# A hand-laid instruction order replaced by another, with eight transfers at most under way, and w_out loaded in four pieces

## The chip, the core and the metric

The kernel runs on one core of a Trainium2 chip. The metric is device time in microseconds (us). The engines are PE (TensorE, matmuls), DVE (VectorE), ACT (ScalarE), POOL (GpSimd) and SP (SyncE, which issues all transfers here). Each runs its own list of instructions strictly in order and waits on semaphores for the others.

## What is computed

Windowed attention over 8 batches, 8 heads, 576 positions, 64 channels a head, and a gated layer on its result:

```python
scores = scale * np.matmul(q, k.transpose(0, 1, 3, 2))
rel = pos[:, None] - pos[None, :]
mask = (rel >= 0) & (rel < 64)
attn = softmax(np.where(mask, scores, -1e9))
x = np.matmul(attn, v)                       # heads side by side: 8 x 576 x 512
for k in range(5):
    gate_pre += conv_w[k] * xp[:, k:k + S, :]
gate = 1.0 / (1.0 + np.exp(-gate_pre))
out = (gate * (x @ w_val)) @ w_out
```

q, k and v are float32; w_val, conv_w and w_out arrive as 64-bit floats, whose two 32-bit words the kernel takes apart itself.

## The kernel before, in words

**Stages.** The work is cut into some 1,500 named pieces. A *pair* is two heads of one batch; `w` numbers groups of two pairs (16 of them, two to a batch), `g` the two halves of a group's query blocks (5 and 4 blocks), `hh` the head of the pair.

- Loads, on SP: `LQi` (q and k of pair i), `LVw` (v of group w, eight transfers), `LW0_0`, `LW0_1`, `LW1_0`, `LW1_1` (quarters of w_val, 512 KB), `LW2`, `LW3` (halves of w_out, 1 MB), `LC` (conv_w), `DO` (stores).
- Attention: `S(w,g)` (scores, PE), `M((w,g),hh)` (add the mask, take the minimum of the negated row, DVE), `X` (exponent and row sum, ACT), `R` (reciprocals, DVE), `N` (normalise; DVE, ACT or POOL), `T` (transpose, DVE), `AVw_0` to `AVw_10` (product with v, PE).
- Splitting of weights into a high and a low part: `w0` to `w3` from w_val, `w4` to `w7` from w_out, `cw` from conv_w; steps `h k b c H p u l r s` on DVE, ACT and POOL (so `w2h` is the first step of w_val's third quarter).
- x: `EXi` copies pair i's result out of PSUM, `XH`, `XL` split it into high and low part.
- Gate: `Ki_y` is the convolution of pairs 0 and 1 of batch 0 on PE (with the diagonals that `DG` builds), copied by `CC`; for all other pairs `Ci_4` is its first tap on ACT, `Ci_3` to `Ci_0` the others on DVE. `SIGb` is batch b's sigmoid, with a change of ACT's function table before and after it.
- Last layer: `Vb_half_jb` (12 matmuls, x by w_val), `HF` (times the gate, DVE), `HH`, `HL` (high and low part of it, ACT and POOL), `Orow` (12 matmuls, output tile), `EO` (copy out of PSUM).

PSUM has two "s" buffers (one S takes both), two "av" buffers (one AV takes both; they come free with `EX` in pairs 0 and 1, with the last tap in the others) and two "f" buffers for `K`, `V` and `O`.

**Order.** A long string, `ORDER`, lists every piece by name in the order in which its instructions are written out. A suffix `/A`, `/V`, `/G` picks ACT, DVE or POOL where there is a choice. A word `*5+0` puts five *spare* matmuls of the first kind (128 x 512, written to a buffer that nobody reads; each is two passes on PE) in front of the next piece, `*0+3` three of the second kind. `placed()` reads the string, and the last loop of the kernel emits the pieces one by one; each engine's list is what falls to it.

**Transfers.** Each transfer that SP issues signals one of eight semaphores, in turn. Before a semaphore is taken again SP waits until the transfer that had it has landed, so at most eight are under way and a transfer waits for the one eight places ahead in SP's list.

Of the kernel before, what the change touches and what calls it, by code (L numbers as in the profile page):

```python
# [54 lines left out]
X((1,0),1) w4u w3l/V R(0,1) w4k/V *1+0 S(1,1) N((0,1),1)/G T((0,0),1) M((1,1),1) N((0,1),0)/G T((0,1),1) w4b
M((1,1),0) T((0,1),0) *0+1 AV0_0 AV0_1 AV0_2 w3r/G w4c w3s/V w4p LQ4_0 LW3 LQ5_0 LV1 LW0_1 LQ6_0 LQ7_0 AV0_3
AV0_4 AV0_5 AV0_6 AV0_7 AV0_8 AV0_9 AV0_10 *0+3 S(2,0) X((1,1),0) w4l/V X((1,1),1) R(1,0) R(1,1) EX0/V DG1/G
w5h/A w4H N((1,1),0)/A EX1/A XH0/A w5u XH1/A N((1,0),1)/V w4r/V N((1,0),0)/V w4s/V M((2,0),0) T((1,0),1)
T((1,0),0) M((2,0),1) N((1,1),1)/G XL1 DG0/G XL0 FR0 FR1 K1_0 AV1_0 S(2,1) T((1,1),1) T((1,1),0) M((2,1),0)
M((2,1),1) K1_1 AV1_1 AV1_2 AV1_3 AV1_4 X((2,0),0) X((2,0),1) w1h/A X((2,1),0) CC1_0 X((2,1),1) AV1_5 AV1_6  # L60
AV1_7 AV1_8 AV1_9 AV1_10 w1k/V R(2,0) w5k/V w1b w5b w1c N((2,0),0)/V w5c w1p w5p T((2,0),0) R(2,1) K0_1 S(3,0)
w1H CC1_1 EX2/A EX3/A C2_4 XH2/G C3_4 CC0_1 XH3/A N((2,0),1)/A w1l/V C2_3 M((3,0),0) C3_3 M((3,0),1) K0_0
T((2,0),1) C3_2 S(3,1) M((3,1),0) M((3,1),1) LV2 LQ8_0 LQ9_0 LV3 S(4,0) X((3,0),0) w5H w5l/G w1r/G XL3
N((2,1),1)/G XL2 w1s/G w5r/G w5s/G N((2,1),0)/G LQ10_0 LQ11_0 V0_1_1_0 X((3,0),1) X((3,1),0) CC0_0 X((3,1),1)
w6h/A w7h/A C2_2 C3_1 C2_1 R(3,0) C2_0 T((2,1),1) C3_0 N((3,0),1)/G N((3,0),0)/G M((4,0),0) T((2,1),0) R(3,1)
M((4,0),1) w6k/V w7k/V w6b w7b SIG0_0 w6c w7c HF0_1_1 w6p w7p FX1 FX0 AV2_0 AV2_1 AV2_2 AV2_3 AV2_4 AV2_5 AV2_6
AV2_7 AV2_8 AV2_9 AV2_10 V0_0_2_0 S(4,1) V0_0_3_0 T((3,0),1) HF0_0_2 M((4,1),1) HF0_0_3 T((3,0),0) EX4/A w6u
EX5/A C5_4 w7u C4_4 LV4 LQ12_0 LQ13_0 N((3,1),0)/G HH0_1_1_0/G HL0_1_1_0 w6l/G HH0_0_2_0/A HH0_0_3_0/A HL0_0_3_0
HL0_0_2_0 w7l/G V0_0_0_0 C4_3 M((4,1),0) HF0_0_0 C5_3 C4_2 X((4,0),0) w6H w7H V0_1_0_0 V0_0_1_0 S(5,0) HF0_1_0
# [1014 lines left out]
```

## Time and profile before

| | us |
|---|---|
| median of 3 runs (lowest, highest) | 329.29 (329.21, 330.62) |
| the profiled execution, as timed | 331.42 |
| its span, first to last instruction | 329.6 |
| PE busy | 313.0 |
| DVE busy | 260.3 |
| ACT busy | 246.0 |
| POOL busy | 174.0 |

The rows of the trace are from the profiled execution; its own time is 2.13 us above the median and 1.8 above its span. "Busy" adds up instructions; matmuls overlap and their ends are modelled, so a busy PE is not PE at its peak.

### The profile page before, as it was taken

Reading aid. Unit: us, or ns where it says so; the run is one execution under the profiler, and the core shown is the slowest. Engines: PE = TensorE matmul, PEld = TensorE weight load, DVE = VectorE, ACT = ScalarE, POOL = GpSimd, SP = SyncE. Lnnn points to the kernel's source line nnn. Section 1 sums busy time; section 2 is a strip of 40 time slices with the busy share of each in tenths; the row PEclk is TensorE's granted clock in tenths of the full one; section 3 lists DMA queues with packets and bytes.
Section 4 is the critical chain, followed back from the end, with each engine's and each line's share of the span. In section 5 each row is a group of like instructions: output and inputs, shape, how many; then the busy total and the mean of one; then the engine's idle time right before and its main releaser. Section 6 shows DMA issues by size and latency. Waiting matters only on the chain.

```text
span 329.6 us, 14996 instructions
## 1 busy us (share of the span) xinstructions
PE 313.0 (95%) x6142; PEld 264.2 (80%) x6142; DVE 260.3 (79%) x992; ACT 246.0 (75%) x844; POOL 174.0 (53%) x227
## 2 busy tenths in 40 slices
PE   8966978899999999999999999999999999999996
...
PEclk9976879999999999999999999999999999999999
...
GB/s 229 384 131 291 254 234 136 96 196 33 37 177 196 193 169 122 184 183 152 148 126 191 110 105 189 183 157 2 140 114 116 30 69 64 34 66 32 2 96 95
DMA packets 28228, 45.03 MB, mean 137 GB/s; under 512 B 3968, under 2 KB 15488, under 8 KB 28160
## 3 DMA queue, kind: packets, MB, share of 16 engines
q1 hardware_dynamic: 28160, 44.08, 43.3%
...
HBM read 34.62 MB, written 9.44 MB: 134 GB/s over the span
## 4 chain that ended last, share of the span: by engine, by line
PE 80%; DVE 13%; ACT 5%; issue 2%; POOL 0%; ACTq 0%; POOLq 0%
PE o L918 29%; PE v L852 27%; PE av L610 10%; PE s L521 8%; DVE p L542 4%; DVE gp L808 3%; PE g L777 3%; PE spare L1032 2%; ACT p L552 2%; DVE pts L579 2%; ACT p L571 1%; ACT h_hi L241 1%; PE spare L1034 0%; DVE w4a L424 0%; ACT L552 0%
## 5 line engine op out<-in xcount | busy, mean ns | idle before, releaser
L552 ACT ACTIVATE p<-p,nm 128x96 f32<-128x96 f32 x288 | 103.9, 363 | 7.7 <-DVE nm L542 7.5
L808 DVE SCALAR_TENSOR_TENSOR gp<-av,cw,gp 128x575 f32<-128x575 f32 (+3 forms) x120 | 93.4, 802 | 7.5 <-ACT gp L811 6.7
L852 PE MATMUL v<-xl,wv_hi 128*128 128x288 f32 x256 | 77.6, 303 | 0.7 <-ACT ot L241 0.7
L852 PE MATMUL v<-xh,wv_lo 128*128 128x288 f32 x256 | 75.4, 294 | 0.0
L852 PE MATMUL v<-xh,wv_hi 128*128 128x288 f32 x256 | 75.0, 293 | 0.0
L881 POOL TENSOR_TENSOR h_lo<-hf,h_hi 128x288 fp32r<-128x288 f32 (+2 forms) x80 | 53.9, 690 | 23.5 <-ACT h_hi L241 22.0
L542 DVE CUSTOM_DVE_ANT_0 p<-s,mask 128x96 f32<-128x96 f32 x288 | 54.8, 250 | 7.3 <-PE s L521 7.1
L918 PE MATMUL o<-wo_hi,h_lo 128*128 128x512 f32 (+1 forms) x148 | 59.6, 403 | 0.2 <-DVE hf L863 0.2
L918 PE MATMUL o<-wo_lo,h_hi 128*128 128x512 f32 (+1 forms) x148 | 57.7, 390 | 0.0
L918 PE MATMUL o<-wo_hi,h_hi 128*128 128x512 f32 (+1 forms) x148 | 57.6, 389 | 0.0
L552 ACT ACTIVATION_READ_ACCUMULATOR p<-p,nm 128x1 f32 x288 | 54.2, 188 | 0.0
L852 PEld LDWEIGHTS v<-xl,wv_hi 128*128 128x128 f32 x256 | 48.1, 188 | 4.0 <-ACT ot L241 1.1
L760 POOL TENSOR_TENSOR xl<-x,xh 128x576 fp32r<-128x576 f32 x32 | 46.0, 1445 | 9.9 <-ACT xh L241 9.6
L246 POOL CAST h_hi<-hf 128x288 fp32r<-128x288 f32 (+2 forms) x37 | 14.2, 392 | 66.1 <-DVE hf L863 57.6
L852 PEld LDWEIGHTS v<-xh,wv_hi 128*128 128x128 f32 x256 | 48.2, 188 | 0.6
L852 PEld LDWEIGHTS v<-xh,wv_lo 128*128 128x128 f32 x256 | 48.1, 188 | 0.0
L610 PEld LDWEIGHTS av<-pts,v 32*64 32x64 f32 x2560 | 36.5, 135 | 11.3 <-issue 5.3
L610 PE MATMUL av<-pts,v 32*64 32x96 f32 (+2 forms) x2560 | 39.6, 251 | 6.1 <-DVE pts L579 2.7
L521 PEld LDWEIGHTS s<-ktb,qtb 64*32 64x32 f32 x2304 | 30.7, 108 | 17.4 <-issue 14.5
L521 PE MATMUL s<-ktb,qtb 64*32 64x96 f32 x2304 | 38.9, 255 | 5.2 <-issue 2.7
L863 DVE TENSOR_TENSOR hf<-v,gp 128x288 f32<-128x288 f32 x64 | 28.2, 447 | 18.0 <-PE v L852 13.9
L573 POOL TENSOR_TENSOR p<-p,rc 128x384 f32<-128x384 f32 (+1 forms) x30 | 28.5, 955 | 20.9 <-DVE rc L561 17.6
...
## 6 DMA issues: line engine op xcount, KB each, us to landing
...
st<-in_w_val_dram SPq DMA_DIRECT2D x4, 512.0 KB, 4.1
st<-in_w_out_dram SPq DMA_DIRECT2D x2, 1024.0 KB, 10.2
...
```

What stands on the lines that cost most here:

```text
L246: COPY = {"A": scopy, "V": vcopy, "G": lambda out, in_: nc.gpsimd.tensor_copy(out=out, in_=in_)}
L521: nc.tensor.matmul(sp_t[m, hh][z * Q:z * Q + Q, t, :], lhsT=held("qt", i)[r, c:c + Q], rhs=held("kt", i)[r, c:c + KW], start=True, stop=True)
L542: nc.vector.tensor_tensor_reduce(out=pe[:, t, :], in0=sp_t[u][:, t, :], in1=mask_of(w, n0 + t), scale=-SCALE, scalar=3.0e38, op0=ALU.add, ...
L552: nc.scalar.activation(out=pe[:, t, :], in_=pe[:, t, :], func=AF.Exp, scale=-1.0, bias=nm[:, t:t + 1], accum_out=su[:, t:t + 1])
L573: MUL[e](out=pe, in0=pe, in1=rc.unsqueeze(2).broadcast_to([P, ng, KW]))
L610: nc.tensor.matmul(av_t[w, z // 2][hh * D:(hh + 1) * D, c + lo * Q:c + hi * Q], lhsT=v_t[w][z * Q:z * Q + Q, hh, m % 2, m // 2 - KEYS[th][ ...
L760: SUB[e](out=batch_tile(xl_t, "xl", b, F32R)[:, hp, :], in0=x_t[i // 2][:, i % 2, :], in1=xh_t[b][:, hp, :].bitcast(F32))
L808: nc.vector.scalar_tensor_tensor(out=acc, in0=av(i, 0, S - back), scalar=col, in1=acc, op0=ALU.mult, op1=ALU.add)
L852: nc.tensor.matmul(vp_t[u][:, 0:NH], lhsT=w[:, c, js], rhs=x[:, c, hs], start=(a + z == 0), stop=(a + z == NM - 1))
L863: nc.vector.tensor_mul(out=hf, in0=vp_t.pop(u)[:, 0:NH], in1=gp_t[b][:, jb, hs])
L881: SUB[e](out=h_lo[:, jb, dst:dst + hi - lo], in0=hf_t[u][:, lo:hi], in1=h_hi[:, jb, dst:dst + hi - lo].bitcast(F32))
L918: nc.tensor.matmul(op_t[key][:, 0:cs.stop - cs.start], lhsT=h[:, jb, col:col + P], rhs=w[:, jb, cs], start=(a + z == 0), stop=(a + z == NM ...
```

## The change

The string `ORDER` is another one throughout: the same pieces, in another order, some on other engines, and with other spares. Each 1 MB load of w_out goes out as two transfers of 512 KB. A tuple `lane` is added to the settings; nothing in the kernel reads it. All arithmetic stays.

```diff
     low='NNNNNAAAA',
+    lane=(2200.0, 900.0, 700, 3350, 1.15),
 )
...
-LW1_0 LC LQ0_0 LQ1_0 *5+0 S(0,0) w2h/A w2k/V cwh/A cwk/V w2b cwb w2c cwc w2p cwp w2l/V cwl/V M((0,0),0)
...
+LW1_0 LC LQ0_0 LQ1_0 LW0_0 LW1_1 w2h/V LQ0_1 LQ1_1 w2k/V cwh/A cwk/V w2b cwb w2c cwc cwH w2H w2p cwp w2l/V LQ2_0
+*4+0 S(0,0) cwl/G M((0,0),0) X((0,0),0) w2r/G LQ3_0 M((0,0),1) w0h/V w0k/V w2s/V w0b X((0,0),1) *2+0 S(0,1) w0c
...
             else:
-                nc.sync.dma_start(out=sv[0], in_=src[:, 2 * (n % 2):2 * (n % 2) + 2, :])
+                for y in range(2):
+                    nc.sync.dma_start(out=sv[0][:, y, :], in_=src[:, 2 * (n % 2) + y, :])
```

On PE, the pieces from the first AV on stand like this, word by word from the two strings with everything of other engines left out. Before: `*0+1 AV0 *0+3 S(2,0) K1_0 AV1_0 S(2,1) K1_1 AV1_1..10 K0_1 S(3,0) K0_0 S(3,1) S(4,0) V0_1_1 AV2 V0_0_2 S(4,1) V0_0_3 V0_0_0`. After: `*3+0 AV0 *1+0 S(2,0) *2+0 S(2,1) AV1_0..1 K1_0 AV1_2..10 K0_1 S(3,0) K0_0 S(3,1) K1_1 S(4,0) V0_1_1 AV2_0..4 V0_0_2 AV2_5 S(4,1) AV2_6..10 V0_0_0 V0_0_3`. From there on V, O, S and AV alternate in much the same way in both.

Three places in the engines' lists follow. `DMAHW0` to `DMAHW7` are the eight semaphores.

SP's list around the loads of w_out (`st`), before: LW2, then `v` of LV0, `qtb`/`ktb` of LQ4, LW3, LQ5, and the first of LV1.

```order
L387 DMA st_131<-in_w_out_dram 128x2x1024 [waits DMAHW0_49]
L356 DMA v_276<-in_vw_dram 32x2x320 [waits DMAHW1_49]
...
L356 DMA v_276<-in_vw_dram 32x2x384 [waits DMAHW0_49]
L335 DMA qtb_77<-in_qT_dram 128x576 [waits DMAHW1_49,PE_49]
L336 DMA ktb_81<-in_kT_dram 128x576 [waits DMAHW2_49]
L387 DMA st_517<-in_w_out_dram 128x2x1024 [waits DMAHW3_49]
L335 DMA qtb_78<-in_qT_dram 128x576 [waits DMAHW4_49,PE_49]
L336 DMA ktb_82<-in_kT_dram 128x576 [waits DMAHW5_49]
L356 DMA v_521<-in_vw_dram 32x2x320 [waits DMAHW6_49]
```

And now, from LW2 to the two halves of LW3, which stand behind LV1:

```order
L389 DMA st_131<-in_w_out_dram 128x1024 [waits DMAHW0_49]
L389 DMA st_131<-in_w_out_dram 128x1024 [waits DMAHW1_49]
L357 DMA v_302<-in_vw_dram 32x2x320 [waits DMAHW2_49]
...
L357 DMA v_302<-in_vw_dram 32x2x384 [waits DMAHW1_49]
L336 DMA qtb_77<-in_qT_dram 128x576 [waits DMAHW2_49,PE_49]
L337 DMA ktb_81<-in_kT_dram 128x576 [waits DMAHW3_49]
L336 DMA qtb_78<-in_qT_dram 128x576 [waits DMAHW4_49,PE_49]
L337 DMA ktb_82<-in_kT_dram 128x576 [waits DMAHW5_49]
L385 DMA st_146<-in_w_val_dram 128x4x256 [waits DMAHW6_49]
...
L389 DMA st_879<-in_w_out_dram 128x1024 [waits DMAHW7_49]
L389 DMA st_879<-in_w_out_dram 128x1024 [waits DMAHW0_49]
```

LV0's last transfer waited for the one transfer of LW2 and now waits for LW2's second half; LW3 has moved from ahead of LQ5 to behind LV1.

DVE's list from the last step of w1 that it does (`w1l`) on, before: the first taps of pairs 2 and 3 (`gp`, from `av_0` and `av_1`), and the two mask groups of S(3,0), each of five instructions and their minima, of which the first is shown.

```order
L439 SCALAR_TENSOR_TENSOR w1l<-st_225,w1m 128x512
L808 SCALAR_TENSOR_TENSOR gp_815<-av_0_701,cw,gp_815 128x575
L542 ISA p_0_0_944,nm_0_0_943<-s_0_0_884,mask_89 128x96
...
L808 SCALAR_TENSOR_TENSOR gp_815<-av_1_702,cw,gp_815 128x575
L542 ISA p_0_1_952,nm_0_1_951<-s_0_1_885,mask_89 128x96
```

And now:

```order
L441 SCALAR_TENSOR_TENSOR w1l<-st_146,w1m 128x512
L810 SCALAR_TENSOR_TENSOR gp_902<-av_0_743,cw,gp_902 128x575
L581 STREAM_TRANSPOSE pts_1_915<-p_0_1_685 128x480
L810 SCALAR_TENSOR_TENSOR gp_902<-av_0_743,cw,gp_902 128x574
L544 ISA p_0_0_976,nm_0_0_975<-s_0_0_918,mask_89 128x96
...
L544 ISA p_0_1_983,nm_0_1_982<-s_0_1_919,mask_89 128x96
L581 STREAM_TRANSPOSE pts_0_996<-p_0_0_665 128x480
L810 SCALAR_TENSOR_TENSOR gp_902<-av_1_744,cw,gp_902 128x575
```

Between the first tap and the first mask group of S(3,0) now stand a transpose and pair 2's second tap, and pair 3's first tap has moved behind both mask groups.

ACT's list around the copies of AV1's result (`x<-av`, EX2 and EX3), before; `gp<-g` are the copies `CC`, `gp<-x,cw` the first taps.

```order
L552 ACTIVATE p_1_1_754,sums_65<-p_1_1_754,nm_1_1_753 128x96 x4
L448 CAST wv_hi<-w1a 128x4x128
L241 COPY gp_815<-g_1_759 128x288
L241 COPY x_928<-av_0_701 128x576
L241 COPY x_928<-av_1_702 128x576
L811 ACTIVATE gp_815<-x_928,cw 128x576 x2
L241 COPY gp_815<-g_1_878 128x288
L241 CAST xh_664<-x_928 128x576
L571 ACTIVATE p_0_1_684<-p_0_1_684,rc_0_862 128x96 x5
```

And now:

```order
L573 ACTIVATE p_0_1_685<-p_0_1_685,rc_0_784 128x96 x5
L554 ACTIVATE p_1_1_788,sums_65<-p_1_1_788,nm_1_1_787 128x96 x4
L242 COPY x_899<-av_0_743 128x576
L450 CAST wv_hi<-w1a 128x4x128
L813 ACTIVATE gp_902<-x_899,cw 128x576
L450 CAST wo_hi<-w5a 128x512
L242 COPY gp_902<-g_0_761 128x288
L242 COPY gp_902<-g_1_873 128x288
L242 COPY x_899<-av_1_744 128x576
L573 ACTIVATE p_0_0_665<-p_0_0_665,rc_0_784 128x96 x5
L813 ACTIVATE gp_902<-x_899,cw 128x576
L242 CAST xh_648<-x_899 128x576
```

Pair 2's copy and first tap now go ahead of the copies of the convolution on PE, and pair 3's come five pieces later than pair 2's.

## Rows read from the trace of the kernel before

**Rows 1.** The page: busy time of PE with its share of the span and its instructions; PE's busy tenths and its granted clock, in tenths of full speed, in 40 equal slices of the span (8.24 us each); the chain that ended last, by engine.

```profile
PE 313.0 (95%) x6142; PEld 264.2 (80%) x6142; DVE 260.3 (79%) x992; ACT 246.0 (75%) x844; POOL 174.0 (53%) x227
...
PE   8966978899999999999999999999999999999996
...
PEclk9976879999999999999999999999999999999999
...
PE 80%; DVE 13%; ACT 5%; issue 2%; POOL 0%; ACTq 0%; POOLq 0%
```

**Rows 2.** Busy time by stretches: from and to in us, the stretch's length, then busy us (and instructions) of PE, PE's weight loads, DVE, ACT and POOL, the granted clock of PE as a share of full speed, the share of the DMA engines and GB/s.

```profile
5.00:66.70 61.70, 50.76 (x1288) 35.15 (x1286) 53.89 (x253) 49.82 (x192) 30.06 (x28) 0.89 0.74 222
46.20:51.30 5.10, 5.10 (x101) 3.77 (x96) 0.84 (x3) 3.67 (x8) 3.22 (x4) 0.78 0.76 241
66.70:110.00 43.30, 43.22 (x893) 38.44 (x892) 40.28 (x160) 42.46 (x154) 34.69 (x44) 1.00 0.44 139
70.00:110.00 40.00, 39.92 (x868) 35.14 (x867) 36.98 (x146) 39.83 (x149) 31.59 (x41) 1.00 0.45 142
110.00:200.00 90.00, 89.74 (x2104) 77.80 (x2104) 82.65 (x331) 78.03 (x282) 51.36 (x65) 1.00 0.50 151
200.00:320.00 120.00, 119.09 (x1823) 105.63 (x1822) 80.44 (x235) 73.01 (x215) 55.10 (x77) 1.00 0.26 83
```

**Rows 3.** DVE in order of time: start, duration, instruction; in brackets the idle time before it and what ended that.

```profile
5.48 0.43 DVE L424 TENSOR_SCALAR w2a<-w2m 128x512 int32<-128x512 int32 x1
...
10.12 0.26 DVE L542 CUSTOM_DVE_ANT_0 p<-s,mask 128x96 f32<-128x96 f32 x1 [2.21 <-PE s L521]
...
15.77 1.17 DVE L424 TENSOR_SCALAR w3a<-w3m 128x512 int32<-128x512 int32 x1
...
37.96 1.03 DVE L579 STREAM_TRANSPOSE pts<-p 128x384 f32<-128x384 f32 x2
...
45.57 0.64 DVE L439 SCALAR_TENSOR_TENSOR w1l<-st,w1m 128x512 f32<-128x512 uint32 x1
48.34 0.82 DVE L808 SCALAR_TENSOR_TENSOR gp<-av,cw,gp 128x575 f32<-128x575 f32 x1 [2.12 <-ACT gp L811]
51.30 0.26 DVE L542 CUSTOM_DVE_ANT_0 p<-s,mask 128x96 f32<-128x96 f32 x1 [2.14 <-PE s L521]
...
65.99 0.45 DVE L863 TENSOR_TENSOR hf<-v,gp 128x288 f32<-128x288 f32 x1
```

**Rows 4.** The chain that ended last, in order of time, merged: start, duration, what. "issue" is time in which the engine waited for nothing that the profile shows.

```profile
1.44 7.54 PE spare L1032 x10
8.97 1.17 PE s L521 x67
...
41.78 1.14 PE av L610 x56
42.92 1.86 issue
44.78 1.76 PE av L610 x46
46.54 3.57 PE g L777 x10
```

**Rows 5.** ACT in order of time, as in rows 3.

```profile
46.45 1.18 ACT L241 COPY x<-av 128x576 f32<-128x576 f32 x2 [2.56 <-PE av L610]
...
59.61 0.67 ACT L413 ACTIVATE w6m<-st 128x512 f32<-128x512 f32 x1
...
61.02 1.28 ACT L995 ACT_TABLE_LOAD   x1 [0.18 <-DVE gp L808]
62.31 2.13 ACT L995 ACTIVATE gp<-gp 128x2304 f32<-128x2304 f32 x1
```

**Rows 6.** SP's issues in order of time (start, how long the issue took, which transfer); the time from issue to landing of the ktb loads issued before 6 us; and from the first 25 us the median time to landing of the loads of w_out and w_val.

```profile
3.18 0.43 SPq L336 DMA_DIRECT2D ktb<-in_kT_dram  x1
...
14.66 1.44 SPq L356 DMA_DIRECT2D v<-in_vw_dram  x2
...
20.84 0.56 SPq L356 DMA_DIRECT2D v<-in_vw_dram  x1
...
DMA to landing us min/median/max: 5.4/5.4/5.4
...
st<-in_w_val_dram SPq DMA_DIRECT2D x4, 512.0 KB, 4.1
st<-in_w_out_dram SPq DMA_DIRECT2D x2, 1024.0 KB, 10.2
```

**Rows 7.** PE: the first matmul of the third V product of batch 0 in order of time; then, from the chain, an AV alone, seven V products in a row and five output tiles (72 matmuls: 48 of 512 columns, and 24 of 256, since one tile is computed in two halves).

```profile
66.65 0.40 PE L852 MATMUL v<-xl,wv_hi 128*128 128x288 f32 x1
...
284.76 2.19 PE av L610 x113
...
301.54 11.04 PE v L852 x84
312.58 14.06 PE o L918 x72
```

**Rows 8.** The last `hf` multiplication on DVE and a subtraction `h_lo` on POOL, as in rows 3.

```profile
312.69 0.46 DVE L863 TENSOR_TENSOR hf<-v,gp 128x288 f32<-128x288 f32 x1 [1.11 <-PE v L852]
...
312.44 0.81 POOL L881 TENSOR_TENSOR h_lo<-hf,h_hi 128x288 fp32r<-128x288 f32 x1
```

More of the change, by code (lines that the diff above doesn't have):

```diff
@@ L55 @@
[L55 to L69, printed above, removed]
@@ new lines @@
+*1+0 S(1,0) M((1,0),0) M((1,0),1) X((0,1),1) cws/G w0r/G w0s/G X((1,0),0) *1+0 S(1,1) R(0,1) T((0,0),0) w3c CF
+M((1,1),0) T((0,0),1) N((0,1),0)/G N((0,1),1)/G T((0,1),0) LQ4_0 X((1,0),1) w3p T((0,1),1) M((1,1),1) R(1,0)
+DG1/G LQ5_0 *3+0 AV0_0 AV0_1 w3H w4h/A w3l/V w4k/V AV0_2 AV0_3 X((1,1),0) w3r/V AV0_4 AV0_5 AV0_6 w4b AV0_7
+AV0_8 w4c w3s/V AV0_9 AV0_10 DG0/V w4p w4u N((1,0),0)/A N((1,0),1)/A EX0/A *1+0 S(2,0) X((1,1),1) T((1,0),1)
+T((1,0),0) XH0/G w4l/G R(1,1) LW0_1 LV1 M((2,0),0) w4H w5h/A N((1,1),1)/G X((2,0),0) w5k/V w4r/V M((2,0),1)
@@ new lines @@
+N((1,1),0)/G XL0 w5u X((2,0),1) EX1/V *2+0 S(2,1) FR0 FR1 M((2,1),0) AV1_0 AV1_1 K1_0 AV1_2 w4s/V X((2,1),0)
+XH1/G XL1 T((1,1),1) T((1,1),0) R(2,0) M((2,1),1) w1h/A N((2,0),1)/A X((2,1),1) AV1_3 AV1_4 AV1_5 AV1_6 w1k/V
+w5b w1b w5c AV1_7 AV1_8 AV1_9 AV1_10 w1c w5p w1p R(2,1) w1l/V K0_1 LW3 LQ6_0 LQ7_0 LV2 LQ8_0 LQ9_0 EX2/A w1H
+C2_4 w5H LV3 C2_3 T((2,0),1) XH2/G S(3,0) CC1_0 CC0_1 EX3/A N((2,0),0)/A K0_0 C2_2 M((3,0),0) M((3,0),1) C3_4
+XH3/A X((3,0),0) T((2,0),0) C3_3 XL2 w1r/G N((2,1),1)/G T((2,1),1) w1s/G w5l/G XL3 w5r/G w5s/G N((2,1),0)/G
@@ new lines @@
+S(3,1) K1_1 CC0_0 X((3,0),1) M((3,1),0) X((3,1),0) M((3,1),1) C2_1 C3_2 w6h/A CC1_1 FX1 FX0 S(4,0) C2_0 C3_1
+R(3,0) LQ10_0 LQ11_0 V0_1_1_0 C3_0 N((3,0),0)/G X((3,1),1) w7h/A AV2_0 AV2_1 M((4,0),0) T((2,1),0) AV2_2 SIG0_0
+R(3,1) w6k/V w7k/V w6b M((4,0),1) N((3,0),1)/G AV2_3 AV2_4 V0_0_2_0 AV2_5 S(4,1) AV2_6 AV2_7 AV2_8 AV2_9 w7b
+AV2_10 LQ12_0 w6c w7c w6p w6u N((3,1),0)/G HF0_1_1 V0_0_0_0 w6l/G EX4/A w6H HH0_1_1_0/A T((3,0),0) HF0_0_2
+M((4,1),0) T((3,0),1) HL0_1_1_0 V0_0_3_0 EX5/A HH0_0_2_0/A C5_4 HF0_0_0 w7p M((4,1),1) w7H C4_4 V0_1_0_0 C5_3
@@ new lines @@
+w7u w6r/G HL0_0_2_0 HF0_0_3 C4_3 LV4 LQ13_0 HH0_0_3_0/A w7l/G V0_0_1_0 C5_2 C4_2 HL0_0_3_0 N((3,1),1)/G S(5,0)
+HF0_1_0 C4_1 X((4,0),0) X((4,1),0) HH0_0_0_0/A w7r/G HF0_0_1 C5_1 HH0_0_1_0/A C4_0 X((4,0),1) V0_1_3_0 V0_1_2_0
+C5_0 T((3,1),1) T((3,1),0) X((4,1),1) AV3_0 HL0_0_1_0 HL0_0_0_0 w7s/G AV3_1 R(4,0) HF0_1_2 AV3_2 AV3_3 AV3_4
+w6s/V AV3_5 AV3_6 AV3_7 AV3_8 AV3_9 AV3_10 N((4,0),0)/A HF0_1_3 HH0_1_3_0/A EX6/A HH0_1_2_0/A O128_0_0 R(4,1)
+M((5,0),1) N((4,0),1)/G HH0_1_0_0/G T((4,0),1) M((5,0),0) T((4,0),0) C6_4 EX7/A HL0_1_3_0 HL0_1_0_0 C6_3
@@ new lines @@
+HL1_0_0_0 HH1_0_3_0/G S(6,1) EO0_0/V C9_1 X((6,0),0) X((5,1),1) R(5,1) XH9/G C9_0 HF1_0_1 HH1_0_3_1/G XL9
+HH1_0_0_1/A HL1_0_3_0 N((5,1),0)/G HH1_0_1_0/A N((5,1),1)/A HH1_0_1_1/G HL1_0_3_1 HL1_0_0_1 V1_0_2_0 DO0_0
+LQ16_0 LQ17_0 LV6 X((6,0),1) T((5,0),0) M((6,1),1) M((6,1),0) V1_1_0_0 HF1_0_2 X((6,1),0) V1_1_2_0 HF1_1_0
+T((5,1),0) R(6,0) C8_2 HH1_1_0_0/A N((6,0),1)/A HL1_0_1_0 HH1_0_2_0/G HL1_0_2_0 HL1_0_1_1 HL1_1_0_0 HH1_0_2_1/G
+V1_1_1_0 S(7,0) HF1_1_2 C8_1 HH1_1_2_0/A V1_1_3_0 T((6,0),1) HF1_1_1 HL1_0_2_1 HL1_1_2_0 HH1_1_1_0/G HL1_1_1_0
@@ new lines @@
+AV7_9 AV7_10 S(9,1) V2_1_0_0 HH2_0_0_0/G HH2_0_1_0/G N((8,0),1)/G N((8,0),0)/G N((8,1),0)/A HH2_0_3_0/G
+HL2_0_0_0 X((9,0),0) HL2_0_3_0 HL2_0_1_0 EX14/V EX15/V T((8,0),0) T((8,0),1) M((9,1),0) HF2_1_0 T((8,1),1)
+V2_0_2_0 V2_1_2_0 X((9,0),1) X((9,1),0) C15_4 C14_4 HF2_0_2 M((9,1),1) R(9,0) HF2_1_2 N((9,0),0)/A HH2_1_2_0/A
+X((9,1),1) HH2_1_0_0/G HL2_1_0_0 HH2_0_2_0/G HL2_0_2_0 T((8,1),0) C14_3 V2_1_3_0 N((9,0),1)/G XH14/G XH15/A
+DO640_0 LQ20_0 LQ21_0 LV8 LQ22_0 LQ23_0 DO512_0 LV9 HF2_1_3 S(10,0) M((10,0),1) M((10,0),0) X((10,0),0) V2_1_1_0
@@ new lines @@
+HL3_0_1_0 HL3_0_2_0 HL3_0_2_1 HL3_1_0_0 AV9_5 AV9_6 AV9_7 AV9_8 AV9_9 AV9_10 T((10,1),1) EX18/V V3_1_2_0
+M((12,0),1) HF3_1_2 HH3_1_2_0/G HL3_0_1_1 HL3_1_2_0 V3_1_3_0 V3_1_1_0 C18_4 R(11,1) C18_3 C18_2 HF3_1_3
+HH3_1_3_0/G EX19/A X((12,0),0) C19_4 X((12,0),1) O1792_0_0 N((11,0),0)/A HL3_1_3_0 HF3_1_1 HH3_1_1_0/G HL3_1_1_0
+O2048_0_0 C19_3 C19_2 XH18/G XH19/A C18_1 C19_1 T((11,0),0) C18_0 C19_0 XL19 N((11,0),1)/A EO1792_0/A S(12,1)
+SIG4_0 AV10_0 AV10_1 AV10_2 EO2048_0/V R(12,0) LQ28_0 DO1792_0 DO2048_0 LV11 AV10_3 XL18 N((12,0),0)/G XL16
@@ new lines @@
+X((14,1),0) HF4_1_1 T((13,0),1) X((13,1),1) C22_1 C23_2 M((14,1),1) O2432_0_0 EO2432_0/A HH4_1_1_0/A CB4 FX11
+FX10 S(15,0) O2304_0_0 C23_1 C22_0 R(14,0) R(13,1) N((13,1),0)/V C23_0 HH4_1_3_0/A HH4_1_2_0/A HL4_1_2_0
+N((14,0),0)/A HL4_1_3_0 SIG5_0 HL4_1_1_0 AV12_0 AV12_1 AV12_2 T((13,1),0) AV12_3 EO2304_0/V AV12_4 DO2432_0
+DO2304_0 LV13 AV12_5 AV12_6 AV12_7 AV12_8 AV12_9 AV12_10 O2560_0_0 M((15,0),1) T((14,0),0) N((13,1),1)/G
+T((13,1),1) HF5_0_0 M((15,0),0) EX24/A N((14,0),1)/V C24_4 HH5_0_0_0/A C24_3 EX25/A C25_4 EO2560_0/A C24_2
@@ new lines @@
+HL5_0_2_1 V5_1_1_0 HF5_1_1 T((14,0),1) EX27/A V5_1_2_0 HL5_1_3_0 O2944_0_0 C27_4 C26_4 C26_3 C27_3 C26_2 XH26/A
+HF5_1_2 T((14,1),1) C26_1 M((15,1),0) C26_0 T((14,1),0) XL24 XH27/G C27_2 C27_1 C27_0 T((15,0),1) XL27
+HH5_1_1_0/A HH5_1_0_0/A EO2944_0/A HH5_1_2_0/A XL26 HL5_1_2_0 CB5 FX12 FX13 HL5_1_1_0 HL5_1_0_0 O2816_0_0
+EO2816_0/A DO2816_0 DO2944_0 V6_0_0_0 SIG6_0 O3328_0_0 AV14_0 AV14_1 AV14_2 EO3328_0/V AV14_3 AV14_4 AV14_5
+AV14_6 AV14_7 AV14_8 AV14_9 AV14_10 EX28/A HF6_0_0 V6_0_2_0 HF6_0_2 EX29/V O3200_0_0 V6_0_3_0 XH28/A X((15,1),0)
```

139 lines of the change are left out of this document (54 added, 85 removed).

## The prediction

> **What bounds the kernel now.** The page of the profile came first. TensorE (PE) is busy for 95% of the span and the chain that ended last runs on PE for 80% of it, but the 40 slices split the program in two [rows 1]: from slice 9 on PE reads 9 almost throughout, before that 6 to 9, with its granted clock down to 6 tenths. The table by stretches [rows 2] puts numbers on it. From 66.7 to 320 us PE lacks 0.08 + 0.26 + 0.91 = 1.25 us of 253.3: there nothing but fewer or shorter matmuls would help. In the first 66.7 us the reader should look at the DVE column instead: between 5 and 66.7 us it is busy 53.89 of 61.7 us, and 4.26 of the 7.8 us that it lacks lie in one stretch, 46.2 to 51.3. PE is no limit there, since it has time for filler matmuls (the "spares"). So the kernel is a start-up paced by DVE, then a long dense stretch paced by PE. The end moves with the moment at which the dense stretch starts.
>
> That moment can be named. The first two V products of batch 0 fill both "f" buffers of PSUM, so the third needs the first `hf` multiplication (HF0_1_1 in the order), which DVE starts at 65.99 [rows 3]; the third V product follows on PE at 66.65 [rows 7]. Ahead of it V0_1_1, V0_0_2, all of AV2 and S(4,1) are done. In the new order the third is V0_0_0, and ahead of it stands exactly the same set. So the difference of the two times for the third V product is the difference of the kernels, up to what changes inside the dense stretch.
>
> **The big gap.** After `w1l` (45.57) DVE waits 2.12 us for ScalarE (ACT) before C2_3 at 48.34, then 2.14 more for scores [rows 3]. The chain tells why [rows 4]: PE is in AV1 at 41.78, loses 1.86 us as "issue" in the middle of it, and ends it at 46.54; so ACT copies AV1 only at 46.45, after 2.56 us of waiting [rows 5]. AV1 began its second piece so late because K1_1 stood ahead of it. Then K0_1 takes 3.57 us [rows 4], at a granted clock of 0.78 in that stretch [rows 2], and S(3,0) sits behind it.
>
> **The change, part by part.**
>
> *Front.* The first spares are eight passes instead of ten; ten took 7.54 us, so PE would reach S(0,0) 1.5 us earlier. S(0,0) also needs the fourth q/k load, issued at 3.18, and a ktb load of these takes 5.4 us to land [rows 6]: 8.6, against 8.97 in the chain [rows 4]. A landing faster by 0.7 is possible, one that is no cover at all too. Gain 0 to 1.1, I take 0.7; DVE waits 2.21 us for just this [rows 3]. Its extra `w2h` (0.4 us) falls into that wait.
>
> *DVE's load up to HF0_1_1.* I compared the two lists of DVE instructions. Masked scores, reciprocals, transposes and convolution steps are the same 18, 8, 12 and 8 groups. Only before: two small pieces of conv_w, `w4l`, the copy EX0 and three normalisations; only after: `w2h`, `w2s`, `w3r`, DG0, EX1 and `w6p`. With 0.4 us for a one-input pass, 0.6 to 0.7 for a two-input one and 0.8 for DG0, which has no row (nearest: the tap of 575 elements) [rows 3], about 3.7 stand against 3.8: nothing, within 1 us either way.
>
> *The gap itself.* At C2_3 the new order has about 1.0 us less DVE work behind it (a transpose of 0.6 and some of the above come later). So DVE arrives at 46.2 - 0.7 - 1.0 = 44.5. Is C2_3 ready? The last transpose for AV1, T((1,1),0), ends at 39.0 now [rows 3]; it moves to 39.0 - 0.7 + 1.3 = 39.6, since 1.3 us more DVE work lies ahead of it. AV1's remaining nine steps now follow K1_0 directly and take at most the 2.2 us of a whole AV [rows 7], so they end at 41.8, not 46.5. ACT then has a half softmax piece to finish (to 42.0), EX2, `w1H` and the first tap: 42.0 + 0.6 + 0.6 + 0.8 = 44.0. So C2_3 starts at 44.5 without a wait. K0_1 still stands ahead of S(3,0): 41.8 + 2.6 (3.6 at half clock) + 1.2 = 45.6 to 46.6. That costs nothing only because C2_3, a transpose and C2_2 now cover it until 44.5 + 2.2 = 46.7; without that cover it would be the old 2.1 us. I keep 0.56 for handovers: the gap gives back 3.7 of its 4.26. Bounds: all 4.26; or 1.9, if the 1.86 of "issue" comes back inside AV1 and K0_0, whose cover is 1.8, runs at half clock.
>
> *From there to the third V.* HF0_1_1 would come at 65.99 - 4.4 = 61.6. It also needs the sigmoid, 1.28 of table and 2.13 [rows 5], after C3_0; that ended 0.18 before 61.02 [rows 5], so at 56.5 now, and the sigmoid at 59.9: covered by 1.7 us. On PE, AV2 is cut into pieces around V0_0_2 and S(4,1), and the last ends near 62.4. So the third V starts at 62.5, 4.1 us earlier than 66.65: 0.3 less than the 4.4.
>
> *SP's queue.* A transfer waits for the one eight places ahead. LV0's last piece was issued at 20.84, 4.7 us after the one before it, since it waited until the 1 MB w_out load had landed [rows 6]. The same bytes stand ahead of it now, so I give the two halves no gain: AV0 near 25 in both. The second w_out load moves from ahead of LQ5 and LV1 to behind them; `w6h`, the first to read it, ran only at 59.61 [rows 5]. Cost nothing; its cover is over 10 us.
> The Trainium skill, "DMA: Bandwidth & Descriptors", Rules for kernel authors, speaks against the split: for bandwidth it asks for 1 MiB or more per DMA. By its fit of 2.0 us plus bytes over 436 GB/s (Anatomy of one DMA; made on another issue path) two halves are an estimated 6.4 us against 4.4, and the sum would lose at most 2.0 if LV0's last piece held the path. The trace bears out neither figure: 512 KB landed in 4.1 us and 1 MB in 10.2.
>
> *Dense stretch.* The same products: V 11.04/7 = 1.58 us, output tiles 14.06/5 = 2.81, AV 2.19 [rows 7]. At the end, the second output tile after the last V now needs that V's `h`, while before the third did. The multiplication starts at 312.69 and takes 0.46; with a copy and a subtraction on POOL, at most 0.81 each [rows 8], that is 314.8, and the first tile (from 312.58) lasts to 315.4 [rows 7]. Hidden by 0.6. For new waits in 250 us I add 0.4 (bounds 0 to 3; now 1.25).
>
> **Sum.** The profiled execution took 331.42 us for a span of 329.6: 331.42 - 0.7 - 3.7 + 0.3 + 0.4 = 327.7. The median of the runs shown lies 2.13 below the profiled execution, which gives **325.6**. With every bound good (1.1, 4.26, 1.0 of DVE load) the gain is 6.4: 322.9. With every bound bad (0, 1.9, 1.0 lost, 0.3, 3) 2.4 are lost: 331.7.
>
> **Rivals.**
> *ACT sets the start, or new waits eat the gain (no change).* ACT is full from 70 to 110 us, 39.83 of 40 [rows 2]. Up to the sigmoid it gets 1.25 us more work: three normalisations and a copy come, a normalisation, a copy, two casts and `w2h` leave. With the idle time of now the sigmoid would end at 64.44 + 1.25 = 65.7 [rows 5] and the third V start at 66.2: 0.4 gained, 328.9. For it: that row. Against: before 61 us ACT's idle time is waiting for AV1 and masked scores, which come earlier. Chance 0.18.
> *More than the sum.* If "issue" and half clock vanish, and DVE also loses nothing more to its neighbours (a pass of 0.43 took 1.17 us at 15.77 [rows 3]), the upper bounds hold with that 0.7 on top: 322.2. Chance 0.08.
> *The dense stretch is not dense (slower).* Between HF0_0_0 and HF0_0_3 DVE now has `w7p`, a mask group and a tap, so 0.4 + 0.7 + 0.7 + 0.4 = 2.2 us from one `hf` to the next where V's pace is 1.58. If such an order goes on, PE waits 0.6 per V: after the seventh V the gain of 4.1 is gone, from the tenth on the kernel is over 0.5% slower, at the twelfth it is at 325.6 + 7.2 - 0.4 = 332.4. For it: DVE busy 40.28 of 43.3 us [rows 2]. Against: after batch 0 no weights are left to split. Chance 0.12.
> That the order moves nothing is excluded by the lists.
>
> **Chances.** What a measurement of this kernel can tell from no change is about 0.5%, 1.6 us. Forecast 0.62, more than the sum 0.08: faster 0.70. Same 0.18, slower 0.12. Range 322.3 to 329.8: it leaves out the farthest gain and most of the slower case.
>
> **What would show it.** Right: DVE idle between C2_3 and M((3,0),0) below 0.6; AV1 ending near 41.8; the third V of batch 0 at 62.5; PE idle below 2 us from there to 310. Wrong: AV1 ending after 44, a sigmoid that ends after 62, or PE waits for `hf` between 62 and 110 us.

## The result, and the profile after

The changed kernel is slower: 332.11 us against 330.18 (medians of 8 runs each), ratio 1.0063, interval 1.0034 to 1.0092. The ratio leaves out one run of the kernel before, 334.22 us, which ran in the chip's slower state. Forecast were 325.6 and "faster"; the range ended at 329.8. Yet the two profiled executions, 331.24 us (span 329.4) and 331.42 (span 329.6), show no loss at all. That contradiction is the first thing to explain.

The page of the changed kernel, with the lines that answer to [rows 1]:

```profile
PE 314.3 (95%) x6144; PEld 263.4 (80%) x6144; DVE 258.8 (79%) x985; ACT 245.4 (75%) x845; POOL 180.3 (55%) x241
...
PE   8695999899999999999999999999999999999996
...
PEclk9979699999999999999999999999999999999999
...
PE 77%; DVE 14%; ACT 3%; issue 3%; DMA 2%; SPq 0%; POOL 0%; ACTq 0%; POOLq 0%
```

The table by stretches of the changed kernel, columns as in [rows 2]; the last row runs from the third V product of batch 0 to the last output tiles:

```profile
5.00:66.70 61.70, 53.25 (x1307) 35.82 (x1306) 56.64 (x263) 52.23 (x203) 33.40 (x33) 0.92 0.74 229
46.20:51.30 5.10, 4.90 (x134) 3.46 (x136) 5.10 (x26) 5.10 (x15) 5.02 (x5) 1.00 0.71 201
66.70:110.00 43.30, 42.41 (x885) 37.47 (x885) 40.48 (x144) 40.90 (x151) 34.02 (x45) 1.00 0.49 144
110.00:200.00 90.00, 89.08 (x2095) 76.98 (x2095) 82.42 (x335) 76.67 (x277) 50.92 (x67) 1.00 0.48 144
64.30:311.93 247.63, 245.61 (x4781) 216.66 (x4782) 201.06 (x717) 191.95 (x642) 144.21 (x193) 1.00 0.39 118
```

DVE has no idle time left from 46.2 to 51.3 (5.10 of 5.10, before 0.84). But the dense stretch is less dense: PE lacks 0.89 us from 66.7 to 110 (before 0.08) and 0.92 from 110 to 200 (before 0.26), and from third V to last tiles 247.63 us pass. The same stretch of the kernel before is its row below:

```profile
66.65:312.40 245.75, 244.50 (x4785) 215.78 (x4781) 202.97 (x723) 192.04 (x646) 139.57 (x183) 1.00 0.38 118
```

In this pair the third V comes 2.35 us earlier (64.30 for 66.65, [rows 7]) and the rest takes 1.9 longer. DVE of the changed kernel in order of time, columns as in [rows 3]:

```profile
9.29 0.26 DVE L544 CUSTOM_DVE_ANT_0 p<-s,mask 128x96 f32<-128x96 f32 x1 [1.25 <-PE s L523]
...
34.19 0.26 DVE L544 CUSTOM_DVE_ANT_0 p<-s,mask 128x96 f32<-128x96 f32 x1 [1.67 <-PE s L523]
...
39.10 0.26 DVE L544 CUSTOM_DVE_ANT_0 p<-s,mask 128x96 f32<-128x96 f32 x1 [1.03 <-PE s L523]
...
46.82 0.81 DVE L810 SCALAR_TENSOR_TENSOR gp<-av,cw,gp 128x575 f32<-128x575 f32 x1
...
63.80 0.45 DVE L865 TENSOR_TENSOR hf<-v,gp 128x288 f32<-128x288 f32 x1
```

The first masked scores come 0.83 us earlier than before (10.12). C2_3 starts at 46.82, not at 44.5 as forecast: DVE has stood 1.67 and 1.03 us for the scores S(2,0) and S(2,1). The reason for the first is in the chain of the changed kernel:

```profile
25.42 1.62 PE av L612 x80
27.05 1.06 PE spare L1034 x2
28.10 3.97 issue
32.07 2.08 PE s L523 x70
```

AV0 ends at 27.05 (before at 28.99 + 2.61 = 31.60, row below), and then PE stands 3.97 us ahead of S(2,0) in a wait that the trace gives to nothing. Most of AV0's lead is gone there. PE of the kernel before, in order of time:

```profile
28.99 2.61 PE L610 MATMUL av<-pts,v 32*64 32x96 f32 x112 [2.72 <-DVE pts L579]
```

### The profile page after: what moved, and what is told of

The parts are those of the page before. It is cut to its first block, busy times and chain, and to the rows that moved or that the text cites. A ratio compares the mean times of both kernels' runs of the same rounds, so it can differ in the third digit from the quotient of the medians.

```text
span 329.4 us, 15018 instructions
## 1 busy us (share of the span) xinstructions
PE 314.3 (95%) x6144; PEld 263.4 (80%) x6144; DVE 258.8 (79%) x985; ACT 245.4 (75%) x845; POOL 180.3 (55%) x241
## 4 chain that ended last, share of the span: by engine, by line
PE 77%; DVE 14%; ACT 3%; issue 3%; DMA 2%; SPq 0%; POOL 0%; ACTq 0%; POOLq 0%
PE o L920 30%; PE v L854 27%; PE s L523 9%; PE av L612 8%; DVE p L544 4%; PE spare L1034 3%; ACT p L554 2%; DVE gp L810 2%; DVE pts L581 2%; DMA out_dram<-ot 2%; DVE hf L865 1%; DVE wo_lo L456 1%; ACT ot L242 0%; DVE rc L563 0%; ACT L554 0%
## 5 line engine op out<-in xcount | busy, mean ns | idle before, releaser
L575 POOL TENSOR_TENSOR p<-p,rc 128x384 f32<-128x384 f32 (+1 forms) x36 | 32.9, 923 | 48.3 <-DVE rc L563 43.4
L612 PEld LDWEIGHTS av<-pts,v 32*64 32x64 f32 x2560 | 35.0, 130 | 6.8 <-issue 2.5
L612 PE MATMUL av<-pts,v 32*64 32x96 f32 (+2 forms) x2560 | 38.2, 245 | 1.1 <-issue 0.8
L581 DVE STREAM_TRANSPOSE pts<-p 128x384 f32<-128x384 f32 (+1 forms) x64 | 38.1, 610 | 1.4 <-ACT gp L997 0.7
```

Source lines behind the costliest of these rows:

```text
L575: MUL[e](out=pe, in0=pe, in1=rc.unsqueeze(2).broadcast_to([P, ng, KW]))
L581: nc.vector.transpose(out=pts_t[w, hh][:, n0 * KW:n1 * KW], in_=p_t.pop(u).rearrange("p t k -> p (t k)"))
L612: nc.tensor.matmul(av_t[w, z // 2][hh * D:(hh + 1) * D, c + lo * Q:c + hi * Q], lhsT=v_t[w][z * Q:z * Q + Q, hh, m % 2, m // 2 - KEYS[th][ ...
```

## The experiments

Three theories stood at the beginning: the new start gains and the new remainder loses (1), the starts of the two profiled executions differ by stalls that come and go (2), the split loads cost (3). The new start is the new order up to the third V product, the remainder is all behind it. The excerpts of `ORDER` show the words that differ, whatever line of the string they stand in; that of e1 stands against the changed kernel, that of e2 against the kernel before.

**Halves of each order, and the split alone.** e1_new_start: the old order from the third V on.

```diff
 w6p w6u N((3,1),0)/G HF0_1_1
-V0_0_0_0 w6l/G EX4/A w6H HH0_1_1_0/A T((3,0),0)
+w7p V0_0_3_0 T((3,0),1) HF0_0_2 M((4,1),1) HF0_0_3
...
```

> New order up to the third V product of batch 0, old order for everything behind it (with w_out in four pieces). Theory 1 (the new start is the gain that its trace shows, 64.30 against 66.65 us at the third V, and the new remainder loses it again): 2.0 to 2.4 us faster than before, ratio 0.993. Theory 2 (the start of the two profiled executions differs by stalls of PE that come and go from run to run, so the new start gains nothing on the median): within 0.5 us of before. Theory 3 (the split loads disturb the start): as slow as the changed kernel, ratio 1.006.

e2_old_start, the reverse:

```diff
 AV2_9 AV2_10 V0_0_2_0 S(4,1)
-V0_0_3_0 T((3,0),1) HF0_0_2 M((4,1),1) HF0_0_3
+LQ12_0 w6u N((3,1),0)/G V0_0_0_0 w6l/G EX4/A
...
```

> Old order up to the third V product of batch 0, new order for everything behind it (w_out in two loads of 1 MB). Theory 1 and theory 2 both put the loss into the remainder, where the trace of the changed kernel loses 2.06 us more than before above the bare durations of its pieces: 2 us slower than before, ratio 1.006 (theory 2), and if the new start were worth 2.35 us the remainder would have to lose over 4, ratio 1.012 (theory 1, since the two together are 1.006). Theory 3 (the split): within 0.5 us of before.

e3_split_only (in the kernel before), and e4_new_unsplit (the reverse, in the changed kernel):

```diff
-                nc.sync.dma_start(out=sv[0], in_=src[:, 2 * (n % 2):2 * (n % 2) + 2, :])
+                for y in range(2):
+                    nc.sync.dma_start(out=sv[0][:, y, :], in_=src[:, 2 * (n % 2) + y, :])
```

> The kernel before with one edit: each 1 MB load of w_out as two of 512 KB; the order stays. Theories 1 and 2: within 0.5 us of before. Theory 3 (the split costs a place in the list of eight transfers under way, so loads behind it start later): 1 to 2 us slower, ratio 1.003 to 1.006.

> The changed kernel with w_out in two loads of 1 MB again. Theories 1 and 2: as the changed kernel, ratio 1.006 within 0.002. Theory 3 (the split is what costs): back at the time before or below, ratio 1.000 or 0.993. If the new order was laid out for the split loads and needs them, it is slower still, over 1.008.

Measured against before: e1 1.0049 (1.0016 to 1.0082), e2 1.0044 (1.0005 to 1.0084), e3 1.0001 (0.9959 to 1.0042), e4 1.0026 (0.9993 to 1.0060). Theory 3 falls for the old order: the split alone moves nothing there, within 0.4%. In the new order e4 lies between, and its interval touches both answers, so a cost of the split up to 0.4% stays possible. Theory 1 falls: the new start with the old remainder is no gain. But e1 is not what theory 2 expected either: some 1.6 us slower than before, where at most 0.5 was expected. e2 is near the 1.006 of theory 2. The traces say why the gain is missing. Busy time from 46.2 to 51.3 us (third busy column: DVE), first of e2, then of e3, both with the old start:

```profile
46.20:51.30 5.10, 5.01 (x124) 3.45 (x126) 4.80 (x24) 4.94 (x20) 4.48 (x5) 1.00 0.77 208
```

```profile
46.20:51.30 5.10, 4.72 (x94) 3.45 (x93) 4.69 (x21) 5.01 (x19) 4.48 (x5) 1.00 0.51 153
```

The old start has no gap of 4.26 us there: 0.30 and 0.41.

**The two kernels themselves, again.**

> The kernel before itself, unchanged, as a second profiled execution and as a measure of what comparisons of this kernel can tell. Ratio 1.000 within 0.4%. If the 4.26 us that DVE stood idle from 46.2 to 51.3 us in the first profiled execution were an accident of that execution (the two runs with the old start since then show 0.30 and 0.41 there), it is under 1 us here and the third V product starts at 63.5 to 66; if it belongs to the order, it is about 4 and the third V starts near 66.7.

> The changed kernel itself, unchanged, as a second profiled execution on the chip and in the call of the next two. Ratio 1.006 within 0.3%. PE stands for 1.6 to 4 us ahead of S(2,0), with 472 matmuls of its list done, as in the three traces with the new start so far; the third V product starts at 63.0 to 64.5.

Measured: before against itself 0.9984 (0.9945 to 1.0023); the changed kernel 1.0071 (1.0039 to 1.0103), the loss again. The second trace of before, from 46.2 to 51.3 us and at C2_3:

```profile
46.20:51.30 5.10, 5.03 (x155) 3.69 (x154) 5.10 (x25) 5.02 (x21) 4.47 (x5) 1.00 0.79 252
...
46.86 0.80 DVE L808 SCALAR_TENSOR_TENSOR gp<-av,cw,gp 128x575 f32<-128x575 f32 x1
```

No idle time of DVE, and C2_3 at 46.86, where the changed kernel has it at 46.82. Theory 2 holds for the start: the gap was that execution's, and with it goes the gain. What the gap was worth shows in c1, DVE first, then PE:

```profile
62.27 0.44 DVE L863 TENSOR_TENSOR hf<-v,gp 128x288 f32<-128x288 f32 x1
```

```profile
63.41 1.00 PE L521 MATMUL s<-ktb,qtb 64*32 64x96 f32 x64
64.34 0.40 PE L852 MATMUL v<-xl,wv_hi 128*128 128x288 f32 x1
```

The first `hf` starts 3.7 us earlier than in the first trace of before (62.27 for 65.99), the third V only 2.31: `hf` is done at 62.71, and PE comes to the third V only after V0_0_2 and S(4,1). All traces side by side (us; "last tiles" is the first matmul of the last five output tiles):

| kernel | third V | last tiles | between | span |
|---|---|---|---|---|
| old start, old rest: before | 66.65 | 312.42 | 245.77 | 329.6 |
| c1 (before again) | 64.34 | 310.07 | 245.73 | 327.3 |
| e3 (split) | 65.90 | 312.71 | 246.81 | 330.1 |
| old start, new rest: e2 | 63.63 | 310.08 | 246.45 | 327.3 |
| new start, old rest: e1 | 63.00 | 310.03 | 247.03 | 327.7 |
| new start, new rest: after | 64.30 | 311.93 | 247.63 | 329.4 |
| c2 (after again) | 64.70 | 313.10 | 248.40 | 330.5 |
| e4 (unsplit) | 64.15 | 311.63 | 247.48 | 328.9 |

The old start spreads over 3 us. The rest takes 245.7 to 246.8 in the old kernel (before, c1, e3), 247.5 to 248.4 in the new (after, c2, e4): 1.7 us more on the mean of three each. Of the old three, e3 is the longest by one stall of 0.77 us under "issue" (169.31). The two mixed kernels are between c1 and the changed kernel. e2, with the new rest, has only the second of the two waits that are named below (1.11 us at 132.97). e1, with the old rest, has neither, but it loses its lead: its third V comes 1.34 us earlier than in c1, and behind a wait for a mask that c1 does not have, the output tile that follows comes only 0.45 earlier. PE of e1, then of c1:

```profile
84.09 1.24 PE L519 MATMUL s<-ktb,qtb 64*32 64x96 f32 x78 [0.27 <-DVE nm L540]
85.27 0.50 PE L916 MATMUL o<-wo_hi,h_lo 128*128 128x512 f32 x1
```

```profile
84.56 1.24 PE L521 MATMUL s<-ktb,qtb 64*32 64x96 f32 x80
85.72 0.50 PE L918 MATMUL o<-wo_hi,h_lo 128*128 128x512 f32 x1
```

The last tiles of the two start at 310.03 and 310.07: an early third V alone did not move the end. Single executions rank starts poorly: e1 has the earliest third V of all and 329.50 us as timed, where the median of its runs is 331.54.

**What the wait ahead of S(2,0) is.** It is there in all seven traces with the new start and its spares, 1.66 to 4.26 us long, always with 472 of PE's matmuls done. e6_no_spares takes ten spares out (they write to a buffer that nobody reads):

```diff
-X((0,0),1) *2+0 S(0,1) w0c
+X((0,0),1) S(0,1) w0c
...
-DG1/G LQ5_0 *3+0 AV0_0 AV0_1
+DG1/G LQ5_0 AV0_0 AV0_1
...
```

> The changed kernel without its spare matmuls from the second group on (10 spares; 8 of them, 16 recorded matmuls, stand ahead of S(2,0)). If PE's stall ahead of S(2,0) is a wait for instructions at a fixed place of its list, it moves with the list: 456 matmuls would be done ahead of S(2,0), PE does about 16 of S(2,0)'s 80 and stands after about 472, for 1 to 4 us. If it is a wait for data or a buffer, it stays ahead of S(2,0)'s first matmul, with 456 done. Time: more half clock without the spares, ratio 1.00 to 1.02.

Measured: 1.0081 (1.0046 to 1.0115). PE of e6 in order of time:

```profile
28.92 0.57 PE L518 MATMUL s<-ktb,qtb 64*32 64x96 f32 x15
32.26 1.59 PE L518 MATMUL s<-ktb,qtb 64*32 64x96 f32 x65 [2.77 <-issue]
```

and matmuls done (first count of the row) up to two moments of the wait in the changed kernel, then up to its end in e6:

```profile
0.00:28.15 28.15, 23.56 (x472) 12.24 (x473) 22.88 (x123) 19.63 (x85) 12.44 (x26) 0.94 0.87 276
0.00:32.00 32.00, 23.56 (x472) 12.24 (x473) 26.70 (x129) 23.48 (x99) 14.17 (x28) 0.94 0.84 258
```

```profile
0.00:32.20 32.20, 19.15 (x471) 11.91 (x472) 25.93 (x128) 22.72 (x98) 13.39 (x28) 0.72 0.87 253
```

PE did 15 of S(2,0)'s 80 matmuls and then stood at 471: the wait kept its place in PE's list and left the operation. Data or a buffer would have held the first matmul. A wait for instructions does just this (the last section has the packets that bring them, and a count that leaves little else). The 1.86 us of "issue" inside AV1 [rows 4] is its relative:

```profile
0.00:42.90 42.90, 35.22 (x726) 21.24 (x727) 36.07 (x181) 31.94 (x135) 18.76 (x29) 0.88 0.85 255
0.00:44.70 44.70, 35.23 (x726) 21.24 (x727) 37.87 (x185) 32.93 (x137) 18.76 (x29) 0.89 0.84 250
```

726 is 254 further on. In c1 no such wait stood there; in e9 (below) it did, and the gap of DVE with it.

**What the new remainder loses.** PE of the changed kernel has two named waits above 0.5 us:

```profile
69.89 0.40 PE L854 MATMUL v<-xl,wv_hi 128*128 128x288 f32 x1 [0.54 <-DVE hf L865]
...
134.36 0.40 PE L854 MATMUL v<-xl,wv_hi 128*128 128x288 f32 x1 [0.81 <-ACT ot L242]
```

Ahead of the first, DVE has `w7p`, four masks (of which one is shown) and a tap between two `hf`; ahead of the second, ACT runs five exponents of another pair (the last is shown) before the output copy that frees the "f" buffer:

```profile
66.41 0.41 DVE L865 TENSOR_TENSOR hf<-v,gp 128x288 f32<-128x288 f32 x1
66.75 1.28 DVE L435 TENSOR_SCALAR w7m<-w7a 128x512 int32<-128x512 int32 x1
67.95 0.24 DVE L544 CUSTOM_DVE_ANT_0 p<-s,mask 128x96 f32<-128x96 f32 x1
...
68.66 0.81 DVE L810 SCALAR_TENSOR_TENSOR gp<-av,cw,gp 128x575 f32<-128x575 f32 x1
69.39 0.44 DVE L865 TENSOR_TENSOR hf<-v,gp 128x288 f32<-128x288 f32 x1
```

```profile
133.38 0.36 ACT L554 ACTIVATE p<-p,nm 128x96 f32<-128x96 f32 x1
...
133.74 0.56 ACT L242 COPY ot<-o 128x512 f32<-128x512 f32 x1
```

e5_new_mended moves two words of the new order; e7 has the first edit alone, e8 the second:

```diff
-V0_1_0_0 C5_3 w7u w6r/G HL0_0_2_0 HF0_0_3 C4_3
+V0_1_0_0 HF0_0_3 C5_3 w7u w6r/G HL0_0_2_0 C4_3
...
-XL12 X((8,0),0) EO640_0/A X((8,1),0)
+XL12 EO640_0/A X((8,0),0) X((8,1),0)
```

> The changed kernel with two words of its order moved: the hf multiplication HF0_0_3 ahead of a convolution tap (C5_3) on DVE, and the output copy EO640 ahead of the exponents X((8,0),0) on ACT. If the loss of the dense stretch lies in the waits that the trace names, the waits of 0.54 us at 69.9 (for hf) and 0.81 to 1.14 at 131 to 134 (for the output copy) go, and the kernel is 1.3 to 1.7 us faster than the changed one: ratio to before 1.001 to 1.002. If other waits come in their place, ratio 1.006 as the changed kernel.

> The changed kernel with only HF0_0_3 moved ahead of the tap C5_3 on DVE. If each named wait is worth its length, 0.5 us faster than the changed kernel: ratio to before 1.005. If the 2.1 us that the two moves together gave hang on this one (each wait early in the dense stretch shifts all that follows against DVE and ACT), ratio 1.001 to 1.002. The wait of 0.54 us at 70 us is gone in either case, that for the output copy near 131 to 135 stays at 0.8 to 1.1.

> The changed kernel with only EO640 moved ahead of the exponents X((8,0),0) on ACT. If each named wait is worth its length, 1.1 us faster than the changed kernel: ratio to before 1.003 to 1.004. If most hangs on this one, 1.001 to 1.002. The wait of 0.8 to 1.1 us near 131 to 135 us is gone, that for hf at 70 us stays at 0.54.

Measured: e5 1.0007 (0.9971 to 1.0042), 0.64% below the changed kernel as measured with it (c2, 1.0071); e7 1.0056 (1.0030 to 1.0082), e8 1.0031 (1.0002 to 1.0061). PE's named waits from the third V to the last tiles, first of the changed kernel, then of e5 (engine and line <- what was waited for: total us, times, longest):

```profile
PE v L854 <- ACT ot L242: 1.0, 2, 0.8
PE v L854 <- DVE hf L865: 0.7, 2, 0.5
PE s L523 <- DVE nm L544: 0.4, 1, 0.4
```

```profile
PE v L849 <- DVE hf L860: 0.4, 2, 0.3
PE s L518 <- DVE nm L539: 0.3, 1, 0.3
```

The stretch shrinks to 246.07 us in e5, to 247.02 in e7 and 247.10 in e8, from 247.63. By the ratios the first move gives 0.5 us and the second 1.3, each uncertain by about 1.4; by the traces each gives 0.5 to 0.6. Only the two together are clear of noise (2.1 us by the ratios), and they bring the changed kernel back to the time before.

**The same repair in the old order.** e9_old_mended:

```diff
-T((12,0),1) HF4_0_3 V4_0_2_0
+HF4_0_3 T((12,0),1) V4_0_2_0
...
-S(13,1) O1664_0_0
+EO1920_0/V S(13,1) O1664_0_0
...
-M((13,1),0) EO1920_0/V C21_1
+M((13,1),0) C21_1
```

> The kernel before with two words of its order moved in the same way: HF4_0_3 ahead of a transpose on DVE, and the output copy EO1920 ahead of the scores S(13,1) and of what DVE does behind them. Its trace has waits of 0.23 us (for hf, 203.8) and 0.67 us (for the output copy, 211.5) there, 0.49 and 0.96 above the bare durations. If a named wait in the dense stretch is worth its length, 1.0 to 1.4 us faster than before: ratio 0.996 to 0.997. If the old order makes them good elsewhere, ratio 1.000.

Measured: 0.9991 (0.9957 to 1.0026): too small to tell, and 1.0 to 1.4 us are just within the interval. The stretch took 245.54 us, 0.2 less than in before and c1, though both named waits are gone; by the trace the forecast of 1.0 to 1.4 failed, and the old order had largely made them good elsewhere. Its start shows once more what the old gap is. PE, then DVE of e9:

```profile
43.83 1.17 PE L605 MATMUL av<-pts,v 32*64 32x96 f32 x72 [1.36 <-issue]
```

```profile
46.87 0.82 DVE L803 SCALAR_TENSOR_TENSOR gp<-av,cw,gp 128x575 f32<-128x575 f32 x1 [1.10 <-ACT gp L806]
49.16 0.26 DVE L537 CUSTOM_DVE_ANT_0 p<-s,mask 128x96 f32<-128x96 f32 x1 [1.47 <-PE s L516]
```

The stall in AV1 and the gap of DVE behind it appear together (before: 1.86 and 4.26 us; e9: 1.36 and 1.10 + 1.47) and are absent together (c1, e2, e3). With the new start the stall alone does not open the gap: e1 has it in AV1, and no idle DVE (5.10 of 5.10) from 46.2 to 51.3. So the cover that the new order puts there works:

```profile
42.59 1.09 PE L608 MATMUL av<-pts,v 32*64 32x96 f32 x65 [1.40 <-issue]
```

## Why the prediction was wrong

**The gap (3.7 forecast).** The step that failed. It priced an accident of one execution as a property of the order. Its own text had the sign: the chain gave 1.86 us of AV1 to "issue", a wait without a cause. The forecast laid AV1's lateness to K1_1 instead and took the whole gap, 4.26 less handovers, as curable. Of the four other traces of the old start three have 0.0 to 0.41 us of idle DVE in these 5.1 us, and only e9, with the stall, has 2.2 (2.95 busy). Without the gap the old order has its third V at 63.63 to 65.90 (c1, e2, e3), not at 66.65: most of the 4.1 us that the new start was to gain there lay in that one execution. C2_3 stands at 46.86 in c1, at 46.82 in the changed kernel.

**The step from the profiled execution to the median (2.13).** The same stall was counted twice. The profiled execution of before lay 2.13 us above its median; the sum took out the gap and then the 2.13 as well. c1, the same kernel without the gap, was 2.34 us faster as timed (329.08 for 331.42), nearly all of it at the third V (2.31): in this pair the gap and the excess over the median are the same time. Other things make an execution slow too: that of e3, without the gap, lay 1.7 us above its median, that of e9, with a smaller one, on it.

**Front (0.7).** Right in the pair (10.12 to 9.29). Over the traces the first mask starts at 9.08 to 10.40 (five old starts, mean 9.94) and 9.01 to 10.45 (seven new ones with spares, mean 9.61): 0.3.

**SP's queue and AV0 ("near 25 in both").** The split costs nothing in the old order, as said, and a loss of 2.0 us would have been seen: e3's interval ends at 0.4%, 1.4 us. Those 2.0 us were an estimate from the fit of the Trainium skill ("DMA: Bandwidth & Descriptors", Anatomy of one DMA), and e3 does not bear it out. But AV0 ended 4.5 us earlier, and that lead ended in the wait ahead of S(2,0). The chain was followed over DVE alone; that PE would run out of instructions after 472 matmuls was not in it.

**From C2_3 to the third V.** The cover between C2_3 and M((3,0),0) came as forecast, without an idle moment. Everything stood about 2 us too late: AV1 ended at 43.9, not 41.8; the sigmoid at 62.6, not 59.9; `hf` 63.80, not 61.6. Two of the forecast's own signs of being wrong came: a sigmoid that ends after 62, and PE waiting for `hf` at 69.9.

**Dense stretch (0.4).** Measured 1.9 in the pair, 1.7 on the mean. The rival "not dense" named the right place, HF0_0_0 to HF0_0_3 with `w7p`, a mask group and a tap between, and its length of 0.6 (measured 0.54), but expected it in each V; it came once. That the lengths agree is luck: from one `hf` to the next passed 2.98 us (66.41 to 69.39), not the 2.2 of the rival, since `w7p` took 1.28 us instead of 0.42 as in before; why, no run shows. The larger wait, an output copy behind exponents on ACT, was in no rival. The 332.4 of that rival lies beside the 332.11 measured, by another sum.

**The account.** Forecast was 3.7 below the median of before as then known (329.29, three runs), measured 1.9 above that of eight runs (330.18): 5.6 apart. At the third V 4.1 us were forecast, and the traces give the new start a mean lead of 0.6 (65.0 for five old, 64.4 for seven new starts): 3.5, of which the gap is the largest part. The dense stretch is 1.3 (1.7 for 0.4). That leaves 0.8 open, with means of so few traces. Open too is why e1 is 0.5% slower than before (its interval reaches down to 0.2%): its trace, of its fastest run, shows the lead lost and no more, and e5, with the same start, is at 1.0007. The 0.4% of e2 fits a new remainder with one of the two waits.
